# Attention and the first run of weights in four blocks of 384 tokens, x in one tile, y in two, order laid out anew

## The chip, the cores and the metric

The kernel runs on one core of a Trainium2 chip. A core has five engines that run their own instruction streams and wait for each other by semaphores: TensorE (PE, matrix products, with a weight-load stream PEld beside it), VectorE (DVE), ScalarE (ACT), GpSimd (POOL) and SyncE (SP), which here issues every transfer between HBM and the on-chip memory SBUF. Products land in PSUM, from which only DVE and ACT can read. The metric is the device time of one execution in microseconds; less is better.

## What is computed

Three layers, one after the other. Inputs q, k, v are float32, two batches of 8 heads, 768 positions, 64 wide; the matrices are float64.

```python
scores_l = scale * q @ k.T                      # kept where |i - j| < 16
k_sum = max over blocks of 32 of k; v_sum = mean over blocks of 32 of v
scores_s = scale * q @ k_sum.T + log(32)
a = softmax([scores_l, scores_s]);  attn = a @ [v, v_sum]
x = attn as (1536, 512)
h = maximum(x @ w_in, 0);  y = (h * h) @ w_out           # w_in 512x2048, w_out 2048x512
h2 = y @ w2_in                                            # 512x1024
solu = h2 * softmax(h2);  ln = (solu - mean) / sqrt(var + 1e-6) * g_ln
out = ln @ w2_out                                         # 1024x512
```

## The kernel before

**Stages.** Attention works on units: one block of tokens for one pair of heads. There are 16 units, four pairs of heads for each of four token blocks, which are 512, 256, 256 and 512 tokens wide (`TOK`). A unit is taken apart into single steps, each with a letter: `lk`, `lq`, `lv`, `ls` load keys, queries, values and the values to be summed; `y`, `j`, `J` sum the values of blocks of 32 (three adds, a small product, a copy) and `P` places the sums; `k`, `K`, `m` transpose keys, copy them and take the maxima; `q`, `Q` do it for queries; `w` builds the key window; `S` is the score product, `R` adds the mask and takes the minimum of each column of 120, `E` the exponentials, `n` the reciprocal of the sum, `N` the scaling, `T` and `C` a transpose and its copy, `V` the product with the values, `H` and `X` the high and low half of x. `R`, `E`, `n`, `N`, `T`, `C` go by groups of four columns of 120.

**Weights.** The 32 tiles of w_in and w_out arrive as float64 words; `l` loads one (512 KB), and `a` (ACT), `b`, `c`, `d`, `e` (all four DVE) make float32 of it, `F` its high half and `f` its low half. Every product is done as three (high by high, low by high, high by low).

**First layer.** `M` is a step's first product (12 matmuls, line 505), `U` the relu, `G` two squares, `D` the low half, `O` the second product (12 matmuls, line 537) which adds into four PSUM tiles `acc`. A step is one chunk of 128 hidden columns for one token block. The first run takes the first six chunks (12 weight tiles) through the token blocks 512, 256, 256, 512; the two blocks of 256 share one set of `acc`. The second and third run take the other ten chunks through three blocks of 512. `Ya` and `Yd` move `acc` into y (copies in the first run, adds later). There is one `h` tile in PSUM, so `M` waits until the relu before it has read it.

**Last layer.** Twelve tiles of 128 tokens: `z`, `Z`, `i`, `u` for the first, then a loop (`moe2`).

**Order.** All of this is issued by `ORDER`, a table of tokens such as `y0d`: step `y` number 0 on DVE (`a` is ACT, `p` POOL). Each engine runs its steps in the order of the table, so a step that waits holds up everything behind it on its engine. Loads are issued by SP in the table's order too. The raw keys and the values to be summed share two buffers, `kl`: `ls0 lk0 lk1 lk2 ls1 lk3 ls2 lk4 ls3 lk5`, each waiting until the load two before it has been used up.

Of the kernel before, what the change touches and what calls it, by code (L numbers as in the profile page):

```python
# [21 lines left out]
ls0 y0d j0 J0a lk0 k0 K0d l0 lq0 lk1 a0 k1 K1d m0 q0 w0a Q0a b0 c0 d0 e0 l1 F0a a1 S0 R0 E0 lq1 lk2 R1 E1 k2 k3 q1 ls1  # L22
K2d K3d b1 n0 m1 lq2 k4 K4a N0p c1 k5 Q1d T0 lv0 lk3 lq3 lv1 K5d m2 w1a S1 y1p w2a f0d j1 C0d J1a q2 ls2 k6 R2 P0 E2
k7 Q2a n1 N1d K6a T1 C1a n2 N2p lk4 K7d q3 Q3a m3 w3p R3 E3 T2 S2 C2d R4 V0 E4 y2p j2 lq4 H0 l2 R5 E5 n3 N3p k8 a2 K8a
lv2 P1 k9 ls3 X0 K9a T3 C3a n4 N4d T4 C4a S3 w4a d1 V1 b2 c2 d2 J2d n5 N5p lk5 l3 w5a H1 R6 R7 E6 y3p X1 T5 lq5 P2 q4
Q4d e1 e2 C5a lv3 n6 j3 lk6 k10 K10a k11 K11d N6p l4 J3a P3 m4 F1a f1p T6 m5 lv4 E7 n7 N7p F2a S4 R8 C6a a3 b3 lq6 c3
d3 e3 V2 T7 E8 ls4 l5 H2 n8 F3d P4 q5 f2d k12 K12a k13 Q5a S5 N8p X2 C7a V3 w6a a4 K13a R9 q6 b4 c4 H3 lq7 w7a T8 f3p
C8a lv5 Q6d y4p X3 S6 R10 l6 lq8 E9 n9 ls5 a5 d4 e4 M0 U0a b5 c5 N9d P5 j4 J4a q7 Q7d d5 V4 lv6 G0 D0p M1 H4 X4 m6 E10
n10 T9 l7 w8a F4a U1a e5 F5a C9a S7 O0 N10p q8 lk7 lq9 R11 E11 y5d f4d f5p V5 lv7 H5 P6 Q8d j5 J5d l8 lq10 a6 a7 X5 G1
ls6 T10 C10a lv8 b6 c6 d6 e6 F6a b7 S8 R12 w9a M2 n11 P7 N11d D1d l9 q9 Q9a k14 k15 K14a K15a T11 lq11 c7 d7 e7 f6p  # L30
w10a C11d S9 R13 O1 P8 E12 n12 a8 m7 F7a q10 Q10a N12p b8 c8 d8 U2a V6 H6 X6 V7 H7 X7 ls7 lv9 l10 T12 C12d f7p lq12 G2
D2d M3 lv10 a9 b9 e8 c9 d9 e9 E13 n13 V8 H8 P9 w11a F8a U3a X8 N13p F9a a10 S10 R14 E14 f8d f9d O2 T13 C13d q11 q12
Q11a Q12a y6p n14 M4 S11 R15 G3 D3p V9 N14p lv11 U4a G4 M5 H9 w12a X9 T14 U5a lq13 l11 b10 c10 q13 Q13a D4d y7p j6 J6a
P10 C14d M6 d10 e10 F10d f10p S12 R16 R17 E15 U6d O3 w13a l12 V10 M7 a11 b11 c11 d11 e11 F11d f11p H10 X10 lv12 G5 j7
J7a D5d n15 N15d lq14 E16 O4 O5 n16 U7a N16p E17 n17 l13 G6 N17p P11 Ya5 T15 T16 C15a C16a lq15 a12 M8 Yd5 S13 R18 G7
D6p O6 U8d G8 D7p R19 V11 H11 X11 w14a E18 M9 U9d D8d b12 T17 O7 n18 N18d q14 q15 Q14a Q15d M10 C17a T18 C18d S14 O8
# [5 lines left out]
F13a f12p U19d G19 D19d M20 f13p a18 O19 U20a G20 D20d b18 c18 d18 e18 M21 F14a f14d F15a F16a O20 U21d F17d l21 a19
M22 f15d G21 F18a D21p O21 U22a b19 c19 M23 d19 e19 G22 D22d a20 f16p a21 U23d G23 b20 O22 c20 d20 e20 l22 l23 F19d
D23d M24 a22 f17p O23 U24a G24 b21 c21 d21 b22 D24d a23 e21 c22 M25 b23 O24 c23 d22 e22 d23 e23 l24 f18d f19p U25a G25
a24 D25d l25 M26 F20a b24 c24 d24 U26d O25 G26 F21a F22a F23a D26p M27 l26 f20p f21p O26 U27d G27 D27d M28 f22p f23p
U28a a25 b25 a26 b26 O27 G28 e24 D28d l27 M29 O28 c25 c26 d25 d26 U29d G29 D29p e25 e26 M30 U30a O29 a27 l28 l29 G30
# [16 lines left out]
def attn_moe_kernel(ctx, tc, q, k, v, w_in, w_out, w2_in, w2_out, g_ln, out):  # L63
# [46 lines left out]
    xp = lctx.enter_context(tc.tile_pool(name="xp", bufs=NT))  # L110
# [55 lines left out]
    NTA = len(TOK) - 1  # L166
    units = [(t, hp) for t in range(NTA) for hp in range(HP)]

    segs = []
    for t in range(NTA):  # L170
        segs.append([])
        lo = TOK[t]
        while lo < TOK[t + 1]:
            hi = min(TOK[t + 1], (lo // S + 1) * S)
            segs[t].append((lo // S, lo % S, (lo - TOK[t]) // 64, (hi - lo) // 64))
            lo = hi

    def size(t):
        return TOK[t + 1] - TOK[t]

# [112 lines left out]

# [26 lines left out]
    def warm(n):  # L320
# [188 lines left out]
    def width(s):  # L509
        return steps[s][0][2] - steps[s][0][1]  # L510
# [248 lines left out]
```

## Time and profile before

| what | value |
|---|---|
| time, median of 3 runs (lowest, highest) | 501.98 us (500.7, 502.87) |
| profiled execution | 504.72 us |
| its span | 503.0 us |
| PE busy | 473.9 us (94%) |
| DVE busy | 339.0 us (67%) |
| ACT busy | 247.9 us (49%) |
| POOL busy | 116.9 us (23%) |

The profile is of one execution; its own time is 1.7 us over its span and 2.7 us over the median of the runs. A share of busy time is an average over stages that have different limits, so it is read by stretches: who is busy all the time in a stretch sets its pace, and the stretch in which nobody is busy all the time is one of waits. Durations in the trace overlap a little where one instruction starts while the one before it drains, so sums of durations come out somewhat over the busy time.

### The profile page before, as it was taken

To read this page: it belongs to the slowest core of one execution; us is meant where nothing else is said; L and a number is where in the kernel's file an instruction comes from. 1 tells how busy PE (TensorE), PEld (TensorE's weight loads), DVE (VectorE), ACT (ScalarE), POOL (GpSimd) and SP (SyncE) were. 2 spreads that over 40 slices of the span, in tenths; PEclk is the share of its full clock that TensorE was granted. 3 is DMA by queue.
4 is the path that set the end of the run, shared out by engine and by line. 5 is a ranking of instruction groups with operands and counts; after the bars stand their busy time and mean duration, and the time that the engine had idled before them with its cause. 6 is when DMAs were issued, how large, how long until landed. Compare 5 with 4: busy or idle time off the path is not lost.

```text
span 503.0 us, 8088 instructions
## 1 busy us (share of the span) xinstructions
PE 473.9 (94%) x2968; PEld 394.8 (78%) x2968; DVE 339.0 (67%) x756; ACT 247.9 (49%) x576; POOL 116.9 (23%) x134
## 2 busy tenths in 40 slices
PE   3686699999999999999999999999999999999997
PEld 2465477789999888888888888888877888888886
DVE  4777889875785459345237778986778787665560
ACT  3687688777764544435326536465522332222231
POOL 3255432721321331511022302101312112110000
PEclk9788899999999999999999999999999999999999
DMA  9999886486224122333011332330000010000011
GB/s 189 206 233 201 214 206 171 98 156 137 74 60 110 51 83 87 81 94 81 36 43 42 124 124 89 125 125 1 1 1 1 22 42 22 21 22 22 21 43 42
DMA packets 60359, 44.04 MB, mean 88 GB/s; under 512 B 46624, under 2 KB 49184, under 8 KB 60320
## 3 DMA queue, kind: packets, MB, share of 16 engines
q1 hardware_dynamic: 60320, 43.53, 34.9%
q8 instruction: 23, 0.38, 0.3%
q14 instruction: 16, 0.13, 0.1%
HBM read 39.19 MB, written 3.15 MB: 84 GB/s over the span
## 4 chain that ended last, share of the span: by engine, by line
PE 78%; DVE 7%; DMA 4%; issue 4%; POOL 3%; ACT 3%; SPq 2%; POOLq 0%; DVEq 0%; ACTq 0%
PE h L505 25%; PE acc L537 23%; PE po L647 13%; PE h L587 9%; DMA kl<-in_v_dram 2%; PE lt L624 2%; PE at L316 2%; PE at L381 1%; POOL kl L242 1%; DMA qr<-in_q_dram 1%; PE at L361 1%; DVE sm L337 1%; ACT sm L345 1%; DVE wf L444 1%; POOL sm L355 1%
## 5 line engine op out<-in xcount | busy, mean ns | idle before, releaser
L505 PE MATMUL h<-xh,wi 128*128 128x512 f32 (+1 forms) x432 | 131.9, 371 | 0.0
L537 PE MATMUL acc<-gh,wo 128*128 128x512 f32 (+1 forms) x432 | 130.2, 368 | 0.0
L505 PEld LDWEIGHTS h<-xh,wi 128*128 128x128 f32 x432 | 79.3, 190 | 14.5 <-issue 0.8
L537 PEld LDWEIGHTS acc<-gh,wo 128*128 128x128 f32 x432 | 78.7, 188 | 14.3 <-issue 1.0
L505 PE MATMUL h<-xl,wi 128*128 128x512 f32 (+1 forms) x216 | 79.5, 368 | 0.0
L537 PE MATMUL acc<-gl,wo 128*128 128x512 f32 (+1 forms) x216 | 79.2, 367 | 0.2 <-DVE gl L94 0.2
L587 PE MATMUL h<-w,wf 128*128 128x512 f32 x288 | 67.4, 390 | 0.5 <-DVE st L598 0.5
L587 PEld LDWEIGHTS h<-w,wf 128*128 128x128 f32 x288 | 54.0, 188 | 11.9 <-PE lt L624 0.7
L515 ACT ACTIVATE r<-h 128x512 f32<-128x512 f32 (+1 forms) x34 | 19.0, 559 | 63.7 <-PE h L505 62.6
L94 POOL TENSOR_TENSOR gl<-r,gh 128x512 fp32r<-128x512 f32 (+1 forms) x19 | 21.5, 1131 | 117.9 <-ACT r L524 103.4
L523 ACT ACTIVATE gh<-r 128x512 fp32r<-128x512 f32 (+1 forms) x54 | 31.3, 580 | 35.0 <-DVE r L517 26.8
L537 PEld LDWEIGHTS acc<-gl,wo 128*128 128x128 f32 x216 | 40.7, 188 | 7.1 <-DVE gl L94 0.7
L505 PEld LDWEIGHTS h<-xl,wi 128*128 128x128 f32 x216 | 41.0, 190 | 6.3
L94 DVE TENSOR_TENSOR gl<-r,gh 128x512 fp32r<-128x512 f32 (+1 forms) x35 | 25.8, 738 | 23.6 <-ACT r L524 21.8
L597 ACT ACTIVATE st<-h,nm 128x1024 f32<-128x1024 f32 x12 | 13.4, 1117 | 51.1 <-DVE nm L594 51.1
L454 DVE SCALAR_TENSOR_TENSOR wf<-st,wf 128x512 uint32<-128x512 uint32 x48 | 36.5, 763 | 1.0
L345 ACT ACTIVATE sm<-sm,mn 128x120 f32<-128x120 f32 x96 | 36.5, 383 | 0.5 <-DVE mn L337 0.4
L437 ACT ACTIVATE wf<-st 128x512 f32<-128x512 f32 x48 | 31.1, 660 | 8.9 <-DMA st<-in_moe_w_in_dram 6.4
L451 DVE SCALAR_TENSOR_TENSOR wf<-st,wf 128x512 uint32<-128x512 uint32 x48 | 34.3, 718 | 1.1
L524 ACT ACTIVATE r<-r 128x512 f32<-128x512 f32 (+1 forms) x54 | 31.6, 585 | 1.8
L440 DVE TENSOR_SCALAR wf<-wf 128x512 f32<-128x512 f32 x48 | 24.8, 518 | 11.1 <-ACT wf L437 11.0
L610 POOL TENSOR_TENSOR vr<-vr,mhalf 128x1 f32<-128x1 f32 x12 | 6.6, 550 | 105.0 <-DVE vr L609 105.0
(126 smaller groups left out, 755.6 us busy)
## 6 DMA issues: line engine op xcount, KB each, us to landing
st<-in_moe_w_out_dram SPq DMA_DIRECT2D x24, 512.0 KB, 3.4
st<-in_moe_w_in_dram SPq DMA_DIRECT2D x32, 256.0 KB, 4.2
st<-in_moe_w_in_dram SPq DMA_DIRECT2D x8, 512.0 KB, 4.0
kl<-in_v_dram SPq DMA_DIRECT2D x8, 384.0 KB, 4.2
kl<-in_k_dram SPq DMA_DIRECT2D x16, 192.0 KB, 4.5
out_dram<-ob SPq DMA_DIRECT2D x11, 256.0 KB, 2.0
vw<-in_v_dram SPq DMA_DIRECT2D x16, 168.0 KB, 3.9
qr<-in_q_dram SPq DMA_DIRECT2D x16, 128.0 KB, 5.0
```

The lines of the kernel that those rows point to most:

```text
L94: eng.tensor_tensor(out=lo, in0=x, in1=hi.bitcast(F32), op=ALU.subtract)
L345: nc.scalar.activation(out=sm[:, j], in_=sm[:, j], func=AF.Exp, bias=mn[:, j:j + 1], scale=-1.0, accum_out=su[:, j:j + 1])
L437: nc.scalar.activation(out=wf_t[n], in_=st_t[n].rearrange("p (n t) -> p n t", t=2)[:, :, 1], func=AF.Abs)
L440: nc.vector.tensor_scalar(out=wf_t[n], in0=wf_t[n], scalar1=C_LO, scalar2=C_HI, op0=ALU.max, op1=ALU.min)
L451: nc.vector.scalar_tensor_tensor(out=w, in0=st[:, :, 0], scalar=29, in1=w, op0=ALU.logical_shift_right, op1=ALU.bitwise_or)
L454: nc.vector.scalar_tensor_tensor(out=w, in0=st[:, :, 1], scalar=0xC0000000, in1=w, op0=ALU.bitwise_and, op1=ALU.bitwise_or)
L505: nc.tensor.matmul(ps[:, 0:hi - lo], wi[:, wsel, d, :], x[t][:, d, lo:hi], start=(n == 0), stop=(n == 3 * HP - 1))
L523: nc.scalar.activation(out=gh, in_=r, func=AF.Square)
L524: nc.scalar.activation(out=r, in_=r, func=AF.Square)
L537: nc.tensor.matmul(acc_t[e][:, lo:hi], wo[:, wsel, e, :], x, start=(edge(s, -1, 3) and i == 0), stop=(edge(s, 1, 3) and i == 2))
L587: nc.tensor.matmul(h2[:, fs], x[:, c, :], w_t[NW1 + nh * NDC + c][:, wsel, :], start=(n == 0), stop=(n == 3 * NDC - 1))
L647: nc.tensor.matmul(po[:, ds], x[:, cs], w_t[NW1 + 8 + c][:, wsel, ds], start=(n == 0), stop=(n == 3 * NF2 - 1))
```

## The change

Attention's token blocks become four of 384. Groups have three columns of 120 where they had four, so there are 32 of them and not 24. The first run of the first layer goes through the same four blocks of 384, each with its own `acc` set; later runs stay at three blocks of 512. x is one tile of 1536 tokens (high) and one (low) and no longer three of each; y is two tiles of 768 tokens, one for each batch, so that a block of 512 which lies in both is added in two pieces. The last run of a block is now always followed by a move of `acc` (before, the last block of the first run went on into the second run in the same `acc`). The whole table of the order is new, also in which engine does a step that may go to several.

```diff
-ls0 y0d j0 J0a lk0 k0 K0d l0 lq0 lk1 a0 k1 K1d m0 q0 w0a Q0a b0 c0 d0 e0 l1 F0a a1 S0 R0 E0 lq1 lk2 R1 E1 k2 k3 q1 ls1
...
+ls0 lk0 y0p j0 lq0 l0 lv0 q0 k0 k1 lk1 K0d K1d m0 Q0a l1 a0 J0a P0 lq1 w0a b0 c0 d0 e0 F0d f0p lk2 S0 R0 R1 k2 K2d k3
...
-    TB = 512
-    NT = NTOK // TB
+    TB = S // 2
+    NTA = NTOK // TB
     NBLK = TB // 64
+    MB = 512
+    NT = NTOK // MB
...
-    GB = 4
-
-    TOK = (0, TB, S, 2 * TB, 3 * TB)
+    GB = NBLK // 2
...
-    xp = lctx.enter_context(tc.tile_pool(name="xp", bufs=NT))
+    xp = lctx.enter_context(tc.tile_pool(name="xp", bufs=1))
...
-        if size(t) < TB:
-            groups.append((u, [(h, j) for h in range(2) for j in range(2)]))
-        else:
-            groups += [(u, [(h, j) for j in range(GB)]) for h in range(2)]
+        groups += [(u, [(h, j) for j in range(GB)]) for h in range(2)]
...
-            xh[t] = xp.tile([P, HP, TB], F32R, name="xh")
-            xl[t] = xp.tile([P, HP, TB], F32R, name="xl")
+            xh[0] = xp.tile([P, HP, NTOK], F32R, name="xh")
+            xl[0] = xp.tile([P, HP, NTOK], F32R, name="xl")
...
-    HALF = ((1, 0, TB // 2), (1, TB // 2, TB))
-    FULL = tuple((t, 0, TB) for t in range(NT))
-    passes = [(x, 0) for x in FULL[:1] + HALF + FULL[2:]] + [(FULL[t], ph) for ph, t in ((1, 2), (1, 1), (1, 0), (2, 0), (2, 1), (2, 2))]
+    HALF = [(t * TB, t * TB + TB) for t in range(NTA)]
+    FULL = [(t * MB, t * MB + MB) for t in range(NT)]
+    passes = [(x, 0) for x in HALF] + [(FULL[t], ph) for ph, t in ((1, 2), (1, 1), (1, 0), (2, 0), (2, 1), (2, 2))]
...
+        for b in range(lo // S, (hi - 1) // S + 1):
+            if b not in y_t:
+                y_t[b] = (yp if b == 0 else rp["p"]).tile([P, NDC, S], F32, name="y", bufs=1)
+            p, q_ = max(lo, b * S), min(hi, b * S + S)
+            for i in range(2):
+                e = 2 * i + part if first else 2 * part + i
+                y, a = y_t[b][:, e, p - b * S:q_ - b * S], acc_t[e][:, p - lo:q_ - lo]
+                if first:
+                    (act_copy, dve_copy)[part](y, a)
+                else:
+                    nc.vector.tensor_tensor(out=y, in0=a, in1=y, op=ALU.add)
```

Three places of the new order. In the rows, a line number is that of the file the row is of; then the operation, what it writes, what it reads, its shape, and how often it stands in a row.

The first instructions of TensorE, before (`acc<-kl,sel` is `j0`, `acc<-ident,kl` transposes keys, `acc<-ident,qr` queries, `at<-kw,qT` is the score product of the first unit):

```order
L249 MATMUL acc_154<-kl,sel 24x128
L199 MATMUL acc_161<-ident,kl 128x128 x3
L199 MATMUL acc_177<-ident,kl 128x128 x3
L225 MATMUL acc_183<-ident,qr 128x128 x4
L316 MATMUL at<-kw,qT_104 64x120 x16
```

and after:

```order
L243 MATMUL acc_157<-kl,sel 24x128
L219 MATMUL acc_168<-ident,qr 128x128 x3
L193 MATMUL acc_172<-ident,kl 128x128 x3
L193 MATMUL acc_176<-ident,kl 128x128 x3
L306 MATMUL at<-kw,qT_104 64x120 x12
```

The queries' transposes went ahead of the keys'; `j0` stays first, but its input is now added up on POOL (`y0p`), not on DVE (`y0d`).

VectorE where the first token block's result leaves PSUM, before (`su` is the sum of a group's exponentials, `y<-acc` is `Yd5`, `sm,mn<-at,strip` the mask step `R`):

```order
L350 TENSOR_SCALAR su<-su 128x4
L351 RECIPROCAL su<-su 128x4
L676 COPY y<-acc_944 128x512
L676 COPY y<-acc_946 128x512
L337 ISA sm,mn<-at,strip 128x120
L337 ISA mn 128x1
```

and after (`sm<-sm,su` is the scaling `N`, `xl<-at,xh` is `X8`, the three `kl<-kl` are `y6`, `pt<-at` a copy `C`):

```order
L343 TENSOR_SCALAR su<-su 128x3
L344 RECIPROCAL su<-su 128x3
L348 TENSOR_TENSOR sm<-sm,su 128x360
L96 TENSOR_TENSOR xl<-at,xh 128x384
L236 TENSOR_TENSOR kl<-kl 96x2x256
L236 TENSOR_TENSOR kl<-kl 96x2x128
L236 TENSOR_TENSOR kl<-kl 96x2x64
L665 COPY pt<-at 120x384
L665 COPY y<-acc_919 128x384
L665 COPY y<-acc_921 128x384
```

Between the last product of block 0 (`O5`) and the copies that free its `acc`, DVE now has a scaling, an `X`, a sum of values and a copy to do.

TensorE around the first product of the first layer (`h<-xh,wi`), before:

```order
L381 MATMUL acc_754<-pt,vw_106 64x64 x16
L225 MATMUL at<-ident,qr 128x128 x2
L361 MATMUL at<-ident,sm 120x128 x4
L316 MATMUL at<-kw,qT_104 64x120 x8
L505 MATMUL h<-xh,wi 128x512
L505 MATMUL h<-xl,wi 128x512
```

and after (`at<-ident,sm` is a transpose `T`):

```order
L354 MATMUL at<-ident,sm 120x128 x3
L306 MATMUL at<-kw,qT_105 64x120 x12
L374 MATMUL acc_731<-pt,vw_106 64x64 x12
L219 MATMUL at<-ident,qr 128x128 x3
L354 MATMUL at<-ident,sm 120x128 x3
L193 MATMUL at<-ident,kl 128x128 x3
L496 MATMUL h<-xh,wi 128x384
L496 MATMUL h<-xl,wi 128x384
```

The score product of a later unit (`at<-kw,qT`) no longer stands between the fourth unit's `V` and the first product; it comes after that product.

## Rows read from the trace of the kernel before

**Rows 1.** The page: busy time by engine; granted clock in 40 slices, tenths of full speed.

```profile
PE 473.9 (94%) x2968; PEld 394.8 (78%) x2968; DVE 339.0 (67%) x756; ACT 247.9 (49%) x576; POOL 116.9 (23%) x134
...
PEclk9788899999999999999999999999999999999999
```

**Rows 2.** Stretches: length, busy PE, PEld, DVE, ACT, POOL (instructions), clock, DMA, GB/s.

```profile
0.00:58.15 58.15, 34.76 (x413) 26.86 (x413) 42.46 (x150) 39.07 (x129) 26.84 (x52) 0.87 1.05 205
...
100.90:157.94 57.04, 56.87 (x636) 52.38 (x636) 38.05 (x133) 40.12 (x131) 15.22 (x16) 1.00 0.51 102
157.94:381.00 223.06, 222.23 (x995) 183.76 (x995) 146.88 (x244) 103.05 (x174) 44.01 (x34) 1.00 0.23 71
...
68.00:95.00 27.00, 25.43 (x218) 19.85 (x217) 25.88 (x75) 22.20 (x68) 9.33 (x9) 1.00 0.68 159
...
0.00:112.00 112.00, 87.03 (x849) 67.58 (x850) 89.01 (x292) 79.19 (x250) 46.14 (x70) 0.92 0.88 186
...
58.15:112.00 53.85, 52.27 (x441) 40.73 (x438) 46.55 (x142) 40.12 (x122) 19.30 (x18) 0.98 0.70 165
```

**Rows 3.** The chain that ended last, in order of time: start, length, engine, tile, line, instructions.

```profile
58.22 4.07 PE h L505 x12
...
109.07 5.68 PE acc L537 x24
...
122.35 1.44 PE acc L537 x12
...
177.18 2.72 PE acc L537 x12
```

**Rows 4.** Timeline of the first 8 us, one row each from DVE, POOL, PE, SP.

```profile
4.74 1.46 DVE L242 TENSOR_TENSOR kl<-kl 96x512 f32<-96x512 f32 x3 [3.40 <-DMA kl<-in_v_dram]
...
5.13 0.10 POOL L673 MEMSET kT<- 128x16 f32 x1
...
6.83 1.54 PE L199 MATMUL acc<-ident,kl 128*128 128x128 f32 x6
...
6.93 0.96 SPq L190 DMA_DIRECT2D kl<-in_k_dram  x2
```

**Rows 5.** DVE's instructions by line and shape: count, busy, mean ns, idle time before.

```profile
L440 DVE TENSOR_SCALAR wf<-wf 128x512 f32<-128x512 f32 x48 | 24.8, 518 | 11.1 <-ACT wf L437 11.0
...
L94 DVE TENSOR_TENSOR wo<-wf,wo 128x512 fp32r<-128x512 f32 x9 | 7.6, 855 | 2.4 <-ACT wo L679 2.4
...
L350 DVE TENSOR_SCALAR su<-su 128x4 f32<-128x4 f32 x24 | 5.0, 210 | 4.0 <-ACT sm L345 3.8
...
L355 DVE TENSOR_TENSOR sm<-sm,su 128x480 f32<-128x480 f32 x7 | 4.6, 657 | 0.2
L351 DVE RECIPROCAL su<-su 128x4 f32<-128x4 f32 x24 | 4.3, 178 | 0.8
...
L676 DVE CAST wo<-wf 128x512 fp32r<-128x512 f32 x8 | 3.4, 420 | 0.9 <-ACT wf L460 0.8
...
L676 DVE COPY kT<-acc 128x384 f32<-128x384 f32 x6 | 3.2, 552 | 2.7 <-PE acc L199 2.6
...
L242 DVE TENSOR_TENSOR kl<-kl 96x512 f32<-96x512 f32 x2 | 1.9, 945 | 3.4 <-DMA kl<-in_v_dram 3.4
...
L242 DVE TENSOR_TENSOR kl<-kl 96x256 f32<-96x256 f32 x2 | 0.8, 421 | 0.1
...
L242 DVE TENSOR_TENSOR kl<-kl 96x128 f32<-96x128 f32 x2 | 0.6, 286 | 0.1
```

**Rows 6.** The chain at 54 us: one mask step of one column on DVE.

```profile
54.25 0.20 DVE sm L337
```

**Rows 7.** Timeline: a POOL sum, a DVE clamp in it, the same clamp without.

```profile
54.34 2.72 POOL L242 TENSOR_TENSOR kl<-kl 96x512 f32<-96x512 f32 x3
...
54.58 1.30 DVE L440 TENSOR_SCALAR wf<-wf 128x512 f32<-128x512 f32 x1
...
60.79 0.42 DVE L440 TENSOR_SCALAR wf<-wf 128x512 f32<-128x512 f32 x1
```

More of the change, by code (lines that the diff above doesn't have):

```diff
@@ L27 @@
[L27 to L36, printed above, removed]
@@ L42 @@
[L42 to L46, printed above, removed]
@@ L59 @@
+e47 f46p O53 u0 g47 F47a f47p z2 Z2p Yd53 Ya53
 """
@@ L164, in attn_moe_kernel @@
     xh, xl = {}, {}
-    NTA = len(TOK) - 1
     units = [(t, hp) for t in range(NTA) for hp in range(HP)]
[L169 to L176, printed above, removed]
+    segs = [[(t // 2, t % 2 * TB, 0, NBLK)] for t in range(NTA)]
     def size(t):
-        return TOK[t + 1] - TOK[t]
+        return TB
     def kslot(b, hp):
@@ L503, in mm1 @@
         for d in range(HP):
-            for wsel, x in ((0, xh), (0, xl), (1, xh)):
-                nc.tensor.matmul(ps[:, 0:hi - lo], wi[:, wsel, d, :], x[t][:, d, lo:hi], start=(n == 0), stop=(n == 3 * HP - 1))
+            for wsel, x in ((0, xh[0]), (0, xl[0]), (1, xh[0])):
+                nc.tensor.matmul(ps[:, 0:hi - lo], wi[:, wsel, d, :], x[:, d, lo:hi], start=(n == 0), stop=(n == 3 * HP - 1))
                 n += 1
@@ L509, in width @@
     def width(s):
-        return steps[s][0][2] - steps[s][0][1]
+        return steps[s][0][1] - steps[s][0][0]
     def relu(s, e):
-        r_t[s] = gp.tile([P, TB], F32, name="r", bufs=2)[:, 0:width(s)]
+        r_t[s] = gp.tile([P, MB], F32, name="r", bufs=2)[:, 0:width(s)]
         if e == "a":
@@ L528, in mm2 @@
     def mm2(s):
-        (t, lo, hi), c = steps[s]
+        (lo, hi), c = steps[s]
         wo = w_t[c // 2 * 4 + 2 + c % 2].rearrange("p s (c f) -> p s c f", c=NDC)
         gh, gl = g_t.pop(s)
-        if edge(s, -1, 1):
+        if edge(s, -1):
             for e in range(NDC):
@@ L536, in mm2 @@
             for i, (wsel, x) in enumerate(((0, gh), (0, gl), (1, gh))):
-                nc.tensor.matmul(acc_t[e][:, lo:hi], wo[:, wsel, e, :], x,
-                                 start=(edge(s, -1, 3) and i == 0), stop=(edge(s, 1, 3) and i == 2))
+                nc.tensor.matmul(acc_t[e][:, 0:hi - lo], wo[:, wsel, e, :], x,
+                                 start=(edge(s, -1) and i == 0), stop=(edge(s, 1) and i == 2))
     def y_out(s, part):
-        t = steps[s][0][0]
-        first = t not in y_t or y_t[t][1] == s
-        if t not in y_t:
-            y_t[t] = ((yp if t == 0 else rp["p"]).tile([P, NDC, TB], F32, name="y", bufs=1 if t == 0 else NT - 1), s)
-        y = y_t[t][0]
-        for e in (0, 1):
-            if first:
-                e = 2 * e + part
-                (act_copy, dve_copy)[part](y[:, e], acc_t[e])
-            else:
-                e = 2 * part + e
-                nc.vector.tensor_tensor(out=y[:, e], in0=acc_t[e], in1=y[:, e], op=ALU.add)
+        lo, hi = steps[s][0]
+        first = s < PHASE[0] * NTA
+        for b in range(lo // S, (hi - 1) // S + 1):
[9 more added lines that the diff above has]
+                    nc.vector.tensor_tensor(out=y, in0=a, in1=y, op=ALU.add)
     def pool_copy(out, in_):
         nc.gpsimd.tensor_tensor(out=out, in0=in_, in1=one.unsqueeze(2).to_broadcast(list(out.shape)), op=ALU.mult)
-    yorder = [(t, i) for t in range(NT) for i in range(TB // P)]
+    NY = NTOK // P
     yhl = {}
     def ysplit(i):
-        t, j = yorder[i]
         yh = stp.tile([P, NDC, P], F32R, name="wf", bufs=6)
         yl = stp.tile([P, NDC, P], F32R, name="wf", bufs=6)
-        src = y_t[t][0][:, :, j * P:(j + 1) * P]
+        src = y_t[i * P // S][:, :, i * P % S:i * P % S + P]
         nc.scalar.activation(out=yh, in_=src, func=AF.Copy)
```

90 lines of the change are left out of this document (52 added, 38 removed).

## The prediction, made before the changed kernel had run

> **What bounds the kernel now.** I read the busy shares first [rows 1], then the stretches [rows 2], then the chain [rows 3], then single instructions [rows 4 to 7]. PE is busy 94% of the span, but the average hides two different kernels. From 100.9 us on PE does not stop (56.87 of 57.04 us, then 222.23 of 223.06) [rows 2]: there the end can only move if PE's own work changes. Before that it is not so. Up to the first product of the first layer, at 58.15 us, nobody is busy all the time: DVE 42.46, ACT 39.07, PE 34.76 of 58.15 us, PE in part at the lower of its two clock levels (slices with 0.7 and 0.8 granted [rows 1]), and the transfer engines are full (DMA 1.05, 205 GB/s) [rows 2]. From there to 112 us PE is busy 52.27 of 53.85 us, but DVE is close behind with 46.55, and from 68 to 95 us DVE is the fuller of the two, 25.88 of 27 us against 25.43 [rows 2]. So what decides is how much PE work is done when the first token block leaves DVE's hands; after that PE runs through.
>
> I use one checkpoint: in the kernel before, the start of the second product `O5`, which ends block 0. The last two `O`s of that stretch take 5.68 us from 109.07 [rows 3], so `O5` starts at about 112.0. The like point after is the start of `O6`, which needs block 0's `acc` freed by `Yd5`.
>
> **The change part by part.** *PE's work.* The number of matmuls and columns stays; a step's 12 matmuls take 2.72 us at 512 columns and 1.44 at 256 [rows 3]. By the line through both, 384 takes 2.08: the first run's 24 steps of two products are 48 x 2.08 = 99.8 us after, and 24 x 2.72 + 24 x 1.44 = 99.8 before. Bounds: at the price per column of the wide shape 384 takes 2.04 (-1.9 us in all), at that of the narrow 2.16 (+3.8). I take the line, 0. Score products, transposes and value products are as many as before.
>
> *PE's work at the checkpoint.* Counted in the two orders, attention's PE work up to there is the same: 144 score instructions in both, 120 value products in both, 60 and 63 transposes of exponentials, 48 of keys in both. Of the first layer, before has 6 `M` of 512, 2 of 256 and 5 `O` of 512 behind it: 32.8 us. After has 9 `M` and 6 `O` of 384: 15 x 2.08 = 31.2. So after has 1.6 us more left to do: **+1.6**.
>
> *DVE's work up to it.* All twelve weight tiles have to be made in both (block 0 uses all), but a block of 384 gives PE a quarter less to do meanwhile. What differs, count by price [rows 5]: scalings `N` on DVE 5 of 480 columns (0.657) against 11 of 360 (about 0.51): +2.3; reciprocals of sums, 16 against 21 pairs of 0.210 + 0.178: +1.9; sums of values 2 against 3 of 0.945 + 0.421 + 0.286: +1.65; `Yd5`, two copies of 384 at 0.55, not yet due at the point before: +1.1; one low half `f` more (0.855): +0.9; high halves `F` 3 against 5 (0.420): +0.8. Less: key copies 7 against 5 (0.552): -1.1; mask steps 72 against 66 columns at 0.20 [rows 6]: -1.2. Six smaller kinds come to -0.3 together. Sum **+6.0 us**. As a test, the same price list over the whole order before gives 90.7 us up to the checkpoint, and DVE was busy 89.0 [rows 2]. So DVE needs 95.0 us after. POOL has 5.6 us less, ACT 2 us less, neither being full there (46.14 and 79.19 of 112) [rows 2].
>
> *DVE's idle time up to it.* Before: 112.0 - 89.0 = 23.0 us, of which 58.15 - 42.46 = 15.7 ahead of the first product and 53.85 - 46.55 = 7.3 behind it [rows 2]. Ahead: two things move. `y0` goes from DVE, where it ran from 4.74 to 6.20, to POOL, whose constants end at 5.23 [rows 4] and which takes about 2.7 us for such a sum [rows 7]: `j0` can start near 7.9 instead of 6.2. `j0` is first in PE's queue, so the key transposes behind it, at 6.83 before, and the next key load, issued at 6.93 when `j0` had freed its buffer [rows 4], come some 1.6 us later: +1.6 (0 if the transfers hide it). Against it, the loads up to the fourth unit's values are fewer: from the shapes, 8672 KB before and 8096 after, 0.59 MB at 205 GB/s [rows 2]: -2.9 (0 if the chain of the two `kl` buffers sets the pace and not the bytes). Together 15.7 + 1.6 - 2.9 = 14.4. Behind it: DVE is now the scarcer engine, and waits less than 7.3; in the densest stretch it waited 1.1 of 27 us, which would be 2.2 in 54. I take 5, nearer the middle.
>
> *Sum.* 95.0 + 14.4 + 5.0 = 114.4, against 112.0: +2.4; and 1.6 of PE's work left over: +4.0; less 0.6 for the POOL work that no longer disturbs DVE (below): **+3.4 us**.
>
> *What costs nothing.* Eight more DVE instructions for adding a block of 512 in two pieces, and four more adds since every first-run block now leaves `acc`: some 4 us on DVE between 158 and 381 us, where it is busy 146.88 of 223 [rows 2]. The four copies after `O23` are covered by the 2.72 us of the product `M25` [rows 3] that stands ahead of `O24`; without that cover 1.1 us. x in one tile: the order with its waits shows the first product waiting for the pieces it reads and for no later block, so 0.
>
> *A rule weighed.* A DVE clamp took 1.30 us while POOL ran a sum from 54.34 for 2.72 us, and 0.42 without [rows 7], so POOL's work costs DVE time. My price list holds the usual share of it: the clamp's mean is 0.518 [rows 5], 0.1 over its undisturbed length; if the four DVE steps of each of the twelve tiles lose as much, that is 4.7 us on the 46 of POOL, 0.1 per us (an estimate), so 5.6 us less POOL give back 0.6. The Trainium skill (SBUF — State Buffer, SBUF: two separate sides) says that the port pair shared by DVE and GpSimd is an exclusive lock, held for the whole instruction. The trace agrees for that clamp, +0.88 us; by the rule every sum or scaling taken off POOL would free DVE for as long as it blocked it, and that would be the second rival below.
>
> **The rivals.** *Slower still, by the clock.* The first `M` took 4.07 us against 2.72 [rows 3], after the sparse stretch before it: it began at the lower of the two levels, 1.2 GHz, and cost 1.35 more. If DVE starves PE between `M0` and `M3`, the clock may stay down over those five products: at worst each takes twice its 2.08 us, +10.4, at best nothing changes. I take half less what is lost already, 5.2 - 1.35 = about +4: 504.72 + 3.4 + 4 = 512.1. For: a granted clock of 0.7 to 0.8 up to 63 us [rows 1]. Against: from there it is 0.9 and more. The Trainium skill (TensorE: Matmul & The Clock Gate, Part 1) says the same of the cause: throttled is the default state, and activity releases it.
>
> *No change: the lock gives the time back.* In the stretch of [rows 7] 2.72 us of POOL cost DVE 1.30 - 0.42 = 0.88, or 0.32 per us. At that price 5.6 us less POOL give back 1.8 and not 0.6, and with DVE's idle time behind the first product at 3 and not 5 the sum is +3.4 - 1.2 - 2.0 = +0.2: 504.9 for the profiled run. For: DVE's long instructions stand beside POOL's. Against: the mean of a clamp, over all, is only 0.1 above 0.42.
>
> *Faster: the waits go.* What DVE waits for ahead of 58 us are single late inputs in an order that had them badly placed; the fourth `X` stood behind two weight steps, and a score product that waited for DVE stood ahead of the first `M`; both are placed better now. If DVE waits ahead of the first product as little as behind it (7.3 of 53.85 us, 14%, so 8.2 of 58) and behind it 2.2, the checkpoint is at 95.0 + 8.2 + 2.2 = 105.4: -6.6 + 1.6 - 0.6 = -5.6, so 499.1. It gets faster by over 2.5 us once DVE's idle time up to the checkpoint is under 13.5 us, against 23.0 before. For: DVE did run 25.88 of 27 us. Against: the transfers are full until 58 us, and the chain of the two buffers keeps its links.
>
> *It does not do what it says:* some wait makes blocks of 384 run like the old order; no change.
>
> **How the numbers follow.** The profiled execution's 504.72 us is 2.7 over the median, so +3.4 is 508.1 for such a run and **505.4** for the median. Chances: forecast 0.40, clock 0.08, lock 0.24, waits gone 0.26, nothing done 0.02. The bounds of the open terms (PE's price -1.9 to +3.8, idle ahead of the first product -1.6 to +2.9) give the forecast its own range of 502 to 510; up to the clock's rival and down into the faster one (499.1 - 2.7 = 496.4 for the median) the range is 497 to 511. About 0.5%, 2.5 us, is what a measurement can tell from no change. Slower by more: most of the forecast, all of the clock, 0.46; within: the lock, nothing done, the forecast's edge, 0.28; faster: 0.26.
>
> **What would show it.** In the profile after: `M` of 384 in 2.08 us; the first `M` at 54 to 58 us; DVE over 90% busy from there to about 114 us, with PE under 95%; `O6` near 114 us; PE full from then on. It is wrong if `O6` starts before 110 us (the waits went), if PE's 12 matmuls take other than 2.04 to 2.16, or if PE stops again behind 120 us.

## The result, and the profile after

The changed kernel takes 504.44 us (median of 6 runs, 504.24 to 506.23) against 501.71 for the kernel before (6 runs, 500.70 to 503.04): ratio 1.0056, 95% interval 1.0036 to 1.0076. So it is 2.7 us slower, where 505.4 was forecast. The profiled execution took 506.23 us with a span of 504.5, 1.5 us over the span of before. That the sum came close does not mean that its terms did: the checkpoint on which it was built came out on the other side.

The page after: PE's line, DVE's share and the granted clock in 40 slices of the span.

```profile
PE 473.9 (94%) x2968; PEld 404.8 (80%) x2968; DVE 356.1 (71%) x806; ACT 242.8 (48%) x573; POOL 115.0 (23%) x135
...
DVE  2989999985496587414557986977887777665560
...
PEclk9997999999999999999999999999999999999999
```

PE's busy time is 473.9 us, to the tenth what it was [rows 1]. So the whole difference of the spans is time in which PE stands still, and it can be told by stretch. First the kernel after: up to its first product, up to the second product of step 6 (the checkpoint), up to that of step 24, and the rest. The columns are those of [rows 2].

```profile
0.00:54.17 54.17, 32.20 (x336) 23.83 (x336) 41.67 (x148) 32.56 (x108) 21.76 (x49) 0.94 1.07 199
54.17:109.00 54.83, 51.57 (x541) 46.58 (x538) 51.89 (x168) 43.76 (x141) 18.13 (x20) 1.00 0.76 173
109.00:198.54 89.54, 89.54 (x708) 84.92 (x706) 62.37 (x165) 52.87 (x142) 19.73 (x19) 1.00 0.35 92
198.54:504.50 305.96, 300.62 (x1392) 249.43 (x1391) 200.21 (x327) 113.56 (x184) 55.42 (x49) 1.00 0.15 51
```

The kernel before has its first two such stretches in [rows 2]; the other two, from its checkpoint at 112 us, are these:

```profile
112.00:198.94 86.94, 86.77 (x730) 77.66 (x729) 56.55 (x147) 50.78 (x135) 23.66 (x22) 1.00 0.35 85
198.94:503.00 304.06, 300.12 (x1393) 249.58 (x1391) 193.45 (x318) 117.97 (x192) 47.10 (x43) 1.00 0.16 52
```

Length less PE's busy time, before against after: 23.39 and 21.97 up to the first product (-1.4), 1.58 and 3.26 up to the checkpoint (+1.7), 0.17 and 0 up to step 24 (-0.2), 3.94 and 5.34 behind it (+1.4). Together +1.5, the difference of the spans. The checkpoint came at 109.0 us and not at 114.4. From there to step 24 PE had 2.8 us more to do (89.54 against 86.77), so that the start of 3.0 us was nearly used up when step 24 began, at 198.54 against 198.94; the loss behind it, 1.4 us of waits and 0.5 us more of PE's work (300.62 against 300.12), then decided the sign.

Timeline of PE after: the rows that waited, with the wait and its releaser in brackets. Three lie between the first product and the checkpoint, two behind 200 us.

```profile
58.44 0.52 PE L354 MATMUL at<-ident,sm 128*120 128x128 f32 x3 [1.61 <-DVE sm L348]
...
99.62 0.92 PE L374 MATMUL at<-pt,vw 120*64 120x64 f32 x24 [0.63 <-issue]
...
101.57 0.52 PE L354 MATMUL at<-ident,sm 128*120 128x128 f32 x3 [1.03 <-DVE sm L348]
...
231.93 0.50 PE L496 MATMUL h<-xh,wi 128*128 128x512 f32 x1 [0.75 <-ACT r L506]
...
369.47 5.29 PE L579 MATMUL h<-w,wf 128*128 128x512 f32 x22 [0.61 <-POOL wf L96]
```

The first and third wait for a normalisation on DVE; the three sum to 3.27, the 3.26 of the stretch. The two late ones, 0.75 + 0.61, are the 1.4 of the last stretch: the kernel before has no wait at either place. The first of them comes where the first products of steps 31 and 32 stand back to back, so that the second has to wait for the relu of the first. In the kernel before the second product of step 30 stands between them; in the kernel after it needs the accumulators that the adds of step 29 (`Yd29`, L546) free on DVE, and these end at 231.75 us.

The chain that ended last, after: twelve matmuls of 384 columns, twice, and the twelve of 512 columns behind the late wait (start, length).

```profile
102.08 2.11 PE acc L528 x12
...
165.95 2.08 PE h L496 x12
...
231.93 3.01 PE h L496 x12
```

One caution on single profiles. Three profiles with one and the same order up to the first product (the kernel after and two of the experiments below) reach it at 54.2, 52.0 and 52.2 us; in two profiles of slightly edited kernels before it is at 55.10 and 55.15, against 58.15 here. So the early stretch of one profile is uncertain by 2 to 3 us, and what an edit does there is read from medians.

Behind the checkpoint there is no such scatter. From the checkpoint to the end, columns of [rows 2], one row each: the kernel before; its order with the first sum on POOL (an experiment below); the kernel after; the kernel after with three low halves on DVE (also below).

```profile
112.00:503.00 391.00, 386.89 (x2121) 327.25 (x2119) 249.99 (x464) 168.75 (x327) 70.76 (x65) 1.00 0.20 59
```

```profile
108.40:499.40 391.00, 386.81 (x2121) 327.24 (x2119) 249.91 (x464) 168.83 (x327) 70.76 (x65) 1.00 0.21 59
```

```profile
109.00:504.50 395.50, 390.16 (x2099) 334.35 (x2096) 262.58 (x492) 166.43 (x326) 75.14 (x67) 1.00 0.20 60
```

```profile
105.84:501.30 395.46, 390.19 (x2099) 334.35 (x2097) 260.86 (x492) 166.66 (x327) 74.95 (x68) 1.00 0.20 60
```

The three profiles with the order of before take 391.00 to 391.02 us here, the six whose order from here on is that of after 395.46 to 395.58. So the changed kernel loses 4.5 us behind the checkpoint, 3.3 of PE's work and 1.2 of waits, whatever the execution. The profile of before came to its checkpoint late: two others with its order, one edit each, did so at 108.4 and 109.5 us. For an execution as long as the medians, which is 1.7 us over its span, the checkpoint follows (an estimate): 501.71 - 1.7 - 391.0 = 109.0 us before, 504.44 - 1.7 - 395.5 = 107.2 after. So the typical gain up to the checkpoint is 1.8 us and not 3.0, and 4.5 - 1.8 is the 2.7 of the medians. That PE's busy totals are equal to the tenth is then chance: the two other profiles of before have 470.9 and 474.2.

### The profile page after: what moved, and what is told of

Same layout as the page of the kernel before. It is cut to its first block, busy times and chain, and to the rows that moved or that the text cites. A ratio compares the mean times of both kernels' runs of the same rounds, so it can differ in the third digit from the quotient of the medians.

```text
span 504.5 us, 8178 instructions
## 1 busy us (share of the span) xinstructions
PE 473.9 (94%) x2968; PEld 404.8 (80%) x2968; DVE 356.1 (71%) x806; ACT 242.8 (48%) x573; POOL 115.0 (23%) x135
## 4 chain that ended last, share of the span: by engine, by line
PE 73%; DVE 16%; issue 5%; POOL 2%; ACT 2%; POOLq 0%; DVEq 0%; ACTq 0%
PE acc L528 22%; PE h L496 22%; PE po L636 13%; PE h L579 9%; DVE sm L330 2%; DVE wf L445 2%; PE lt L616 2%; DVE wf L442 2%; PE at L306 2%; DVE wf L435 1%; PE at L374 1%; DVE sm L348 1%; PE at L354 1%; DVE wf L431 1%; DVE ks L201 1%
## 5 line engine op out<-in xcount | busy, mean ns | idle before, releaser
L496 PE MATMUL h<-xh,wi 128*128 128x512 f32 (+1 forms) x432 | 133.5, 370 | 0.7 <-ACT r L506 0.7
L528 PE MATMUL acc<-gh,wo 128*128 128x512 f32 (+1 forms) x432 | 132.3, 368 | 0.0
L528 PEld LDWEIGHTS acc<-gh,wo 128*128 128x128 f32 x432 | 80.1, 188 | 10.3 <-issue 0.5
L96 POOL TENSOR_TENSOR gl<-r,gh 128x512 fp32r<-128x512 f32 (+1 forms) x24 | 29.2, 1216 | 139.2 <-ACT r L515 116.6
L506 ACT ACTIVATE r<-h 128x384 f32<-128x384 f32 (+1 forms) x40 | 21.6, 540 | 56.6 <-PE h L496 54.9
L445 DVE SCALAR_TENSOR_TENSOR wf<-st,wf 128x512 uint32<-128x512 uint32 x48 | 38.0, 801 | 1.1
L442 DVE SCALAR_TENSOR_TENSOR wf<-st,wf 128x512 uint32<-128x512 uint32 x48 | 37.6, 786 | 1.2
L96 DVE TENSOR_TENSOR gl<-r,gh 128x512 fp32r<-128x512 f32 (+1 forms) x30 | 19.9, 664 | 15.3 <-ACT r L515 15.2
```

The source lines that it names most:

```text
L96: eng.tensor_tensor(out=lo, in0=x, in1=hi.bitcast(F32), op=ALU.subtract)
L442: nc.vector.scalar_tensor_tensor(out=w, in0=st[:, :, 0], scalar=29, in1=w, op0=ALU.logical_shift_right, op1=ALU.bitwise_or)
L445: nc.vector.scalar_tensor_tensor(out=w, in0=st[:, :, 1], scalar=0xC0000000, in1=w, op0=ALU.bitwise_and, op1=ALU.bitwise_or)
L496: nc.tensor.matmul(ps[:, 0:hi - lo], wi[:, wsel, d, :], x[:, d, lo:hi], start=(n == 0), stop=(n == 3 * HP - 1))
L528: nc.tensor.matmul(acc_t[e][:, 0:hi - lo], wo[:, wsel, e, :], x, start=(edge(s, -1) and i == 0), stop=(edge(s, 1) and i == 2))
```

## The experiments

Each ratio is to runs of the kernel before made beside that experiment, whose median lay between 501.5 and 502.3 us; a difference to the kernel after "by medians" is between such groups of runs, and where the ratios say less than the medians it is named.

Theory A: in the kernel after, DVE's time sets when the first block ends, so a microsecond more or less on DVE (or in the first key transposes) is one more or less at the end. Rivals: the transfers or PE set it; or it is single badly placed waits.

**The first sum of values back on VectorE.**

```diff
-ls0 lk0 y0p j0 lq0
+ls0 lk0 y0d j0 lq0
```

> The changed kernel with one letter of the order put back: the first sum of values, y0, on DVE again and not on POOL. Theory A: in the changed kernel DVE works without a break from its first key copy at 9.97 us to about 105 us, so what starts it later (POOL's sum, 5.20 to 7.78, where the kernel before had DVE's own, 4.74 to 6.20) moves everything up to there: the first key copy comes at about 7.8, the end of block 0 and the whole time fall by 2.0 us, to 502.4. Theory B: the loads set that stretch and DVE is only busy beside them: the time falls by 0 to 0.5 us, since the first loads are issued as before.

503.51 us (7 runs, 502.80 to 504.46), ratio to before 1.0043 (1.0028 to 1.0059): 0.9 less than after by medians, 0.7 by the ratios, whose intervals overlap. Its profile is 2.5 us shorter (span 502.0), first product at 51.6, but by the caution above most of that may be chance. So POOL's longer sum costs some 0.7 to 0.9 us, less than the 1.6 of the prediction and between the two expectations; that it costs more than nothing is likely, but not clear of the noise. The same edit the other way, in the kernel before:

```diff
-ls0 y0d j0
+ls0 y0p j0
```

> The kernel before with its first sum of values, y0, on POOL and not on DVE, as in the change. DVE's first key copy comes at about 9.9 and not 7.8. DVE was idle another 10 us between there and the first product: if that takes it up, 0 to 0.7 us more, 502.0; if every link of the start is handed on to the end, 2.1 more, 503.8.

501.85 (12 runs), ratio 0.9995 (0.9972 to 1.0018): no change that can be seen, though 0.9 us more would still lie in the interval.

**Five useless clamps on VectorE, in either kernel.** Each clamps a weight tile once more than is needed.

```diff
-b5 c5
+b5 b5 b5 b5 b5 c5
```

> The changed kernel with DVE's clamp of weight tile 5, just behind the fourth unit's low half of x, done five times and not once: four more DVE steps of 0.42 us, 1.7 us, that nobody needs. Theory A (DVE sets the time up to 105 us): 1.7 us more, 506.1. Theory B (DVE is only busy beside the loads): under 0.4 more.

> The kernel before with the same clamp of weight tile 5 done five times, just behind the first product. If DVE is as much the limit here as after: 1.7 us more, 503.4. If PE is (busy 52.27 of 53.85 us behind the first product, with DVE idle 7.3): DVE catches up by 112 us, 0 to 0.8 more, 502.1.

After: 508.49 (6 runs), ratio 1.0131 (1.0094 to 1.0167), +4.0, more than either expectation. Before: 503.63 (12 runs), 1.0016 (0.9991 to 1.0040), +0.8 by the ratio, +2.0 at its upper end, and +1.8 by the medians (501.83 beside it). So 1.7 us on DVE cost at least their own length in the kernel after, by the medians over twice that. In the kernel before they cost less than in the kernel after; whether less than their own length is not shown, and neither of that run's two expectations is ruled out. Timeline of PE in the clamps' run of the kernel after, at the first of the three waits, and the stretch behind it (columns of [rows 2]):

```profile
58.42 0.51 PE L354 MATMUL at<-ident,sm 128*120 128x128 f32 x3 [3.43 <-DVE sm L348]
```

```profile
60.00:70.00 10.00, 10.00 (x112) 9.29 (x112) 8.54 (x28) 7.42 (x24) 3.62 (x4) 0.85 0.45 102
```

The wait grew from 1.61 to 3.43, by the clamps' length. Behind it the granted clock is 0.85 over ten microseconds where the kernel after has 1.00: the next product began at the lower level and took 3.82 us, and PE's busy time between its first product and the checkpoint was 53.11 us where it had been 51.57. That is the slower rival's mechanism, in small. It is not tied to the longer wait: in the run with the late places (below), whose order is unchanged up to there, that product took 3.85 us behind a wait of 1.59, and the stretch up to the checkpoint shows a clock of 0.97 and 53.15 us of PE.

**Three sums of values on POOL, to relieve VectorE.**

```diff
-y3d
+y3p
-y5d
+y5p
-y6d
+y6p
```

> The changed kernel with the sums of values y3, y5 and y6 on POOL and not on DVE: 5 us less DVE work ahead of the end of block 0, 8 us more on POOL. Theory A (DVE sets the time up to 105 us): PE has only 3.3 us of idle time between the first product at 54.17 and 109, so up to 3 us less, 501.5. Theory B (loads set it): no change. Theory C (POOL's sums hold DVE up by 0.32 us for each of their own, as the clamp of the kernel before): 8 x 0.32 = 2.6 us of it are lost again, about 1 us less, 503.4.

508.65 (5 runs), ratio 1.0143 (1.0122 to 1.0164): +4.2, outside all three expectations. Timeline of POOL, then of DVE and PE beside it:

```profile
90.97 3.15 POOL L236 TENSOR_TENSOR kl<-kl 96x512 f32<-96x512 f32 x3
...
95.05 3.20 POOL L236 TENSOR_TENSOR kl<-kl 96x512 f32<-96x512 f32 x3
```

```profile
91.33 1.66 DVE L96 TENSOR_TENSOR wo<-wf,wo 128x512 fp32r<-128x512 f32 x1
92.92 0.55 DVE L665 COPY pt<-at 120x384 f32<-120x384 f32 x1
...
93.85 1.52 DVE L431 TENSOR_SCALAR wf<-wf 128x512 f32<-128x512 f32 x1
95.40 1.38 DVE L435 TENSOR_SCALAR wf<-wf 128x512 uint32<-128x512 uint32 x1
...
97.96 1.78 DVE L445 SCALAR_TENSOR_TENSOR wf<-st,wf 128x512 uint32<-128x512 uint32 x1
```

```profile
100.91 0.92 PE L374 MATMUL at<-pt,vw 120*64 120x64 f32 x24 [2.38 <-issue]
...
102.86 0.87 PE L354 MATMUL at<-ident,sm 128*120 128x128 f32 x3 [1.03 <-DVE sm L348]
```

And the stretch around the second wait:

```profile
101.00:105.00 4.00, 2.97 (x32) 2.86 (x33) 3.53 (x15) 2.41 (x9) 0.00 (x0) 0.59 0.31 79
```

Undisturbed, the low half takes 0.68 in the same profile, the two weight steps 0.42 and 0.43, the last 0.69. Beside POOL's sums and low halves they lose 1.0, 1.1, 0.95 and 1.1 us, nearly what moving the sums, 1.46 us each, took off DVE. DVE was busy 85.01 of the first 100 us against 85.86. What was left is the harm: the value products waited 2.38 us in place of 0.63, and behind them the clock fell to 0.59. From its first product to the checkpoint PE stood still 1.7 us longer than in the kernel after and was busy 2.6 us longer (54.21 against 51.57), so the clock took more than the wait. That the sums themselves come later from POOL is not the reason here: the small product that reads the first of the two shown started without a wait at 95.83 us, against 96.29 in the kernel after.

**Three low halves from POOL to VectorE.** This is the reverse.

```diff
-D4p
+D4d
-D5p
+D5d
-D6p
+D6d
```

> The kernel after with three low halves of the first layer's squares (steps 4, 5, 6) on VectorE in place of POOL. In the profile of the kernel after each takes 1.01 to 1.17 us on POOL, at 90.48, 93.73 and 96.89 us, and beside them a VectorE cast took 1.23 us in place of 0.42, a sum of values 2.16 in place of 1.46, a weight step 1.39 in place of 0.69: 2.2 us lost. On VectorE each costs 0.55, 1.65 together. Theory A (POOL's work on SBUF stops VectorE's work on SBUF for as long as it runs): VectorE ends 0.5 us earlier, the time is 0 to 0.6 us lower, and those three instructions are back at 0.42, 1.46 and 0.69. Theory B (the long ones are long for another reason): they stay long, and the time is 1.65 us higher.

503.08 (12 runs, 502.47 to 504.24), ratio 1.0025 (1.0006 to 1.0043): 1.4 less than after. First the rows of the kernel after, POOL and DVE, then DVE in this run (its times are 2 us earlier):

```profile
90.48 1.01 POOL L96 TENSOR_TENSOR gl<-r,gh 128x384 fp32r<-128x384 f32 x1
93.73 1.17 POOL L96 TENSOR_TENSOR gl<-r,gh 128x384 fp32r<-128x384 f32 x1 [2.24 <-ACT r L515]
...
96.89 1.02 POOL L96 TENSOR_TENSOR gl<-r,gh 128x384 fp32r<-128x384 f32 x1 [1.99 <-ACT r L515]
```

```profile
90.54 1.23 DVE L665 CAST wo<-wf 128x512 fp32r<-128x512 f32 x1
...
93.35 2.16 DVE L236 TENSOR_TENSOR kl<-kl 96x512 f32<-96x512 f32 x3
...
97.07 1.39 DVE L445 SCALAR_TENSOR_TENSOR wf<-st,wf 128x512 uint32<-128x512 uint32 x1
```

```profile
91.14 1.46 DVE L236 TENSOR_TENSOR kl<-kl 96x512 f32<-96x512 f32 x3
...
94.16 0.69 DVE L445 SCALAR_TENSOR_TENSOR wf<-st,wf 128x512 uint32<-128x512 uint32 x1
94.89 0.43 DVE L665 CAST wo<-wf 128x512 fp32r<-128x512 f32 x1
```

All three are back at their own length, as theory A here said, although DVE has three instructions more. The wait for unit 19's normalisation went from 1.03 to 0.43 us, the 0.63 ahead of the value products disappeared, and from the first product to the checkpoint it took 53.6 us in place of 54.8. The gain of 1.4 is larger than the 0 to 0.6 expected.

**Two normalisations earlier in VectorE's queue.** No work is taken away; only the two that PE waits for move up.

```diff
-c5 k11 d5 e5 M0 n10 N10d
+c5 k11 n10 N10d d5 e5 M0
...
-E19 R20 R21 E20
+E19 n19 N19d R20 R21 E20
...
-n19 N19d T19
+T19
```

> The kernel after with two normalisations of exponentials earlier in VectorE's queue and nothing else: unit 10's ahead of two weight steps (0.69 + 0.69 us), unit 19's ahead of six mask steps (1.3 us). In the profile of the kernel after PE stops three times between its first product and 109 us: 1.61 us at 56.8 for unit 10's, 0.63 at 99.0, 1.03 at 100.5 for unit 19's. Theory A (these single waits, not VectorE's total work, are what is lost between the first product and the sixth): both waits go below 0.3 us, the second product of step 6 starts 2 to 2.5 us earlier after the first product than the 54.8 us of the kernel after, and the median falls by 1.5 to 2.5 us, to 502 to 503. Theory B (VectorE's work as a whole sets the end of the first block): the waits go, but others of the same length come further on, where the steps that now stand later are waited for, and the time stays within 0.5 us of 504.4.

504.27 (12 runs, 503.82 to 505.21), ratio 1.0030 (1.0003 to 1.0057). By the medians 0.2 less than after. The ratio gives 1.3 less, since the runs of before beside it stood at 502.32. The profile speaks for theory B; PE's waits from the first product on:

```profile
56.04 0.51 PE L354 MATMUL at<-ident,sm 128*120 128x128 f32 x3 [0.16 <-DVE sm L348]
...
58.47 0.44 PE L496 MATMUL h<-xh,wi 128*128 128x384 f32 x1 [1.14 <-DVE r L508]
...
99.35 0.92 PE L374 MATMUL at<-pt,vw 120*64 120x64 f32 x24 [1.49 <-issue]
```

1.61 became 0.16 and 1.03 nothing, as aimed at, but a relu that now stands later is waited for 1.14 us, and the value products 1.49 in place of 0.63. The stretch took 54.5 us, nearly as long as without the edit (54.8). Theory B here fits: the waits are where DVE's lateness shows, not what causes it.

**Eight copies from VectorE to ScalarE,** with the first sum on VectorE.

The letters of the order that change:

```diff
-K2d K3d C0d C1d Q3d F11d C17d Q11d
+K2a K3a C0a C1a Q3a F11a C17a Q11a
```

> The kernel after with the first sum of values on VectorE (as in the run before of that kind, which took 2.5 us off its profile and 0.9 off its median) and eight copies moved from VectorE to ScalarE: two key copies (1.01 us together), two of exponentials (1.01), one of queries (0.55) ahead of the first product, one high half of weights (1.23, beside a POOL instruction), one copy of exponentials and one of queries (1.10) around 90 us. That takes 4.9 us off VectorE and puts about 3.6 on ScalarE, whose waits there are longer than that. Theory A (VectorE sets when the first block ends, and ScalarE has room): the second product of step 6 starts 5 to 7 us earlier than at 109.0, and the time is 5 to 7 us below the kernel after, 497 to 499.5. Theory B (with VectorE relieved the transfers or the order of the other inputs set the pace at once): no more than the 0.9 to 2.5 us of the first sum, 502 to 503.5. Theory C (ScalarE's longer queue makes the exponentials late): slower than 504.4.

503.90 (12 runs), ratio 1.0042 (1.0018 to 1.0065): the same as with the first sum alone. The first product came at 51.8 against 51.6. Rows of PE and of DVE show who is late instead:

```profile
89.80 0.45 PE L496 MATMUL h<-xh,wi 128*128 128x384 f32 x1 [0.31 <-ACT r L506]
```

```profile
97.69 0.17 DVE L343 TENSOR_SCALAR su<-su 128x3 f32<-128x3 f32 x1 [0.89 <-ACT sm L338]
```

So A has a limit: the exponentials go from DVE (masks) to ScalarE and back, and a copy that is given to ScalarE stands ahead of them there; these two rows fit that, no run tests it by itself. Up to the checkpoint DVE was busy 89.0 us where it is 92.4 with the first sum alone, and the checkpoint came 0.2 us earlier (106.2 against 106.4): DVE, although full, is not what sets the time by itself.

**The two late waits.** The adds of step 29 ahead of four weight steps and the product of step 32 behind the second product of step 30; the first normalisation of the last layer behind a weight split. Once alone, once with all the above sums (y3, y5, y6 on POOL and the first on DVE), once with the eight copies.

```diff
-M31 b26 c25 d25 e25 D30d Yd29 U31a M32 l28 O30 U32a
+M31 D30d Yd29 U31a b26 c25 d25 e25 l28 O30 M32 U32a
...
-O53 u0 g47 F47a f47p z2 Z2p
+O53 g47 F47a f47p z2 Z2p u0
```

> The changed kernel with two late places of the order put right: the adds of block 2's result at step 29 ahead of the four weight steps, and the next first product behind the second product again (the gap of 0.75 us at 231 us and the 3.01 us product behind it); and the first tile's layer norm behind the last two low halves, so that POOL doesn't wait for DVE with the last weights behind it (the gap of 0.61 us at 369 us). If these gaps are lost time: 1.6 us less, 502.8. If PE would only wait elsewhere: no change, 504.4.

> All three edits together: y0 on DVE, y3, y5 and y6 on POOL, the two late places put right. Theory A: 2.0 + 2 (less than 3, since PE's idle time gets used up by the first) + 1.6 = 5.6 us less than the changed kernel, 498.8, which is 2.9 under the kernel before. Theory B: only the late places count, 502.8.

> The same as the run with the eight copies on ScalarE, with the two late places moved as in the earlier run of that kind (the adds of step 29 ahead of four weight steps and the product of step 32 behind the second product of step 30; the first normalisation behind the weight split). Theory A: the two gaps behind 200 us are worth what they show in the profile, so 0.5 to 1.2 us below the run with the copies alone. Theory B (gaps only move): the same as that run within 0.5 us.

Alone 503.94 (6 runs), ratio 1.0056 (1.0036 to 1.0076): by the ratio nothing, by the medians 0.5. With the sums 507.91 (4 runs), ratio 1.0125 (1.0106 to 1.0143), with POOL's sums costing no less than alone. With the copies 503.95 (12 runs) against 503.90: nothing. PE's late waits, alone:

```profile
236.72 0.50 PE L496 MATMUL h<-xh,wi 128*128 128x512 f32 x1 [0.69 <-ACT r L506]
```

```profile
374.93 5.72 PE L579 MATMUL h<-w,wf 128*128 128x512 f32 x24 [0.82 <-DVE st L590]
```

The first wait came one step later with 0.69 in place of 0.75; the second went, and one that had been 0.50 became 0.82. Behind 200 us PE stood still 4.99 us in place of 5.34 (before: 3.94). The times can't tell such a gain, but the rows from the checkpoint to the end can. This run:

```profile
108.42:503.30 394.88, 389.89 (x2099) 334.49 (x2096) 261.24 (x492) 166.12 (x326) 74.74 (x68) 1.00 0.20 60
```

The four profiles with the late places have 394.87 to 394.90 us here, where the order of after has 395.46 to 395.58 and the eight copies alone 395.31. So the edit is worth 0.6 us (0.4 beside the copies) of the 4.5, about half of it PE's work and half waits, and not the 1.6 that was aimed at. What would take the rest of the late waits away was not found.

**What helped, together:** the first sum and the three low halves on VectorE, the late places, and the two normalisations.

> The two early normalisations together with what helped before: the first sum of values on VectorE (median -0.9), three low halves on VectorE (-1.4) and the two late places (-0.5). If the gains are of different waits they add: -0.9 - 1.4 - 0.5 and 1.5 to 2.5 for the normalisations, less 0.6 that two of them share at the same wait: 500 to 501.2, so at or below the kernel before (501.5 to 501.8). If VectorE's total work decides, the normalisations give nothing and it is 501.5 to 502.

501.61 (12 runs, 501.17 to 503.05), 2.8 less than after, ratio to before 0.9981 (0.9957 to 1.0005). Against the run with the normalisations alone, on the same chip, it is 2.7 less. From the first product to the checkpoint it took 53.6 us, as the low halves alone, so the normalisations added nothing there. The median meets the expectation by DVE's total work (501.5 to 502); the ratio, put on the 501.7 of before, gives 500.8 and would meet the other. With blocks of 384 the kernel can be brought to where it was, not shown to be faster.

## Why the prediction was right in the time and wrong in the way

That 504.4 came so near to 505.4 is luck: two errors of opposite sign. Up to the checkpoint +2.4 was forecast and came out at -3.0 in the two profiles, some -1.8 by the medians; behind it +1.6 was forecast and came out at +4.5. The 0.6 that I took off for POOL's disturbance is a third error (below).

- *PE's price of 384 columns* was right: 2.08 and 2.11 us per twelve matmuls, the line between [rows 3]'s prices. Behind attention's small products the twelve take 2.28 to 2.31, as those of before then take 2.94 to 2.99 at 512 columns and 1.61 to 1.63 at 256. That PE's total of 473.9 us did not move is no proof of the price, being chance.
- *PE's work left over*, +1.6, was in kind right and too small: 2.8 us more between checkpoint and step 24 and 0.5 behind it, 3.3 together. Which steps make up the other 1.7 was not taken apart. Up to the checkpoint PE had been busy 83.77 us against 87.03 [rows 2], of which 1.35 is the slow first product of before.
- *DVE's work up to the checkpoint* was forecast at 95.0 and was 41.67 + 51.89 = 93.56 at 109.0 us.
- *DVE's idle time* is the step that failed: 14.4 + 5 forecast, 12.5 + 2.94 found. Behind the first product DVE was busy 94.6%; I had taken a value near the middle between 7.3 and 2.2 where its densest stretch, 25.88 of 27 us [rows 2], already showed the end. With 93.56 and 15.44 the checkpoint's rule gives 109.0 + 1.6 - 112.0 = -1.4, so the condition that I had named for being wrong, the second product of step 6 ahead of 110 us, was met, and so was another, PE stopping again behind 120 us. The base was of one late execution, too: the two other profiles of before have 19.7 and 20.9 us of DVE's idle time up to the checkpoint where I took 23.0, and about 5 behind the first product where I took 7.3. The faster rival was half true: the waits went, to 15.4 us and not to the 13.5 from which it decides.
- *What I costed at nothing* helped to make the sign. "Some 4 us on DVE where it is busy 146.88 of 223" [rows 2] argued from an average; at step 29 the adds are late, and PE waits 0.75 us, and with the tail's 0.61 it is 1.4 us. Less the 0.2 us that the kernel before waits ahead of step 24, these are the 1.2 of waits in the 4.5.
- *The share of POOL's disturbance*, 0.1 us of DVE's time per us of POOL, -0.6 in all, was mis-sized: it was an average over work that is disturbed and work that is not. Three low halves of 3.2 us on POOL cost DVE 0.81 + 0.70 + 0.70 us, 0.7 per us; taking them away gained 1.4 us by medians (some 0.2 to 2.9 by the intervals of the ratios) although DVE did them itself. The lock rival was right that the price can be far above 0.1; the changed order put POOL's work beside DVE work that suffers, and how much the 5.6 us less of POOL gave back elsewhere was not measured.
- *The clock* did not fall in the kernel after (1.00 from the first product on), and did in four of the experiments: where a wait grew to 3.43 us, in the two with sums on POOL, where one grew to 2.38, and once with no longer wait.
- The profile's +1.5 and the medians' +2.7 differ by 1.2, all of it ahead of the checkpoint, where the profiled executions were both late, that of before by more. What the size of the block does by itself stays open: blocks of 384 in the old order were not tried.

## What to carry to other kernels

Make a table by stretch, busy and idle time apart, also behind the place that one has argued about, and compare it with a second profile of the same order: a stretch that is the same in both can be trusted to a tenth of a microsecond, and equal busy totals can be chance. An edit that is "covered on average" has to be checked at each place where something waits for it. When an engine is full, as DVE here, moving the wait did not help, and moving the work helps only if the engine that takes it neither blocks the first one nor stands in the same loop of dependences.

## What the runs showed of the hardware that I had not expected

How much POOL costs DVE depends on what DVE does and where its operands are. Beside POOL's work a cast took 1.23 in place of 0.43 us, a weight step with one operand 1.52 in place of 0.42, one with two operands 1.78 in place of 0.69, a sum of values 2.16 in place of 1.46: all of them from SBUF to SBUF. A copy out of PSUM in the middle of a POOL sum took its usual 0.55, and a reduction of one operand in SBUF its usual 0.94 (L201, at 67.40 us in the kernel after, inside a sum of 2.63). The Trainium skill (SBUF — State Buffer, SBUF: two separate sides) says just this more exactly than I had used it: the lock is taken by a DVE instruction in a mode with two ports, or by one with two inputs in SBUF (this only against a GpSimd instruction that reads SBUF), and by GpSimd's instructions; whichever is second blocks. The traces agree in that some kinds lose and others nothing, at some 0.4 to 0.9 us lost per us of overlap; in which mode a DVE instruction ran they do not show. The Trainium skill (Perfetto Trace Analysis, Optimizing Scalar/DVE Operations) also warns that offloading between the two might not help; here it cost 4.2 us.

And a wait of PE can cost more than its length: after one of 3.43 us the next product began at the lower clock level (1.2 GHz), and 1.7 us of added DVE work became 4.0 at the end; how much of the 4.0 is the clock's is open, since in another run it fell as far behind a wait of 1.59 us, and in the kernel after not at all behind one of 1.61.
